# First units of a fused attention and FFN kernel: k copied in two parts, idle matmuls after k removed, intra products ahead of inter products, one natural-k group made last

## The chip, the core and the metric

The kernel runs on one core of one Trainium2 chip. Times are device microseconds (us) of whole executions; a profiled execution has a span (first to last instruction) about 1.7 us shorter than its time. A comparison is given as a median of each kernel and as a ratio.

## The reference

```
# attention: batch 4, 8 heads, 768 positions, head size 64, blocks of 64
intra = (qb @ kb^T) * Dmask          # decay lam^(i-j) below the diagonal
out   = intra @ vb + (qb * lam_pow) @ kv_state
kv_state = lam_block * kv_state + (kb * rev_pow)^T @ vb
# bilinear FFN on the result, x = [3072, 512]
y = ((x @ w_a) * (x @ w_b)) @ w_out  # d_ff = 1536
```

The kernel works in blocks ("units") of 128 positions, 24 of them, and folds the decay into q and k. Groups of one to four units go through the FFN together. The first group has four units, and its attention has to be finished before the FFN can begin. That stretch, the first 20 us, is called the head here.

## The kernel before

In the head, q and k of four units arrive in two loads each. VectorE (DVE) multiplies a load by its decay table in two parts, TensorE (PE) transposes each part with four matmuls against an identity, and ScalarE (ACT) copies the result out of PSUM:

```python
    def load4(w, i):
        ...
        tps = ps_bank("t" + w, [128, 2, PACK, 128], BF16)     # one PSUM bank
        for j in range(2):
            ...                                               # DVE multiplies part j
            for r in range(PACK):
                nc.tensor.transpose(tps[:, j, r, :], ..., ident)
        nc.scalar.copy(xT4[w][:, 2 * i:2 * i + 2, :]..., tps[:]...)   # one copy, both parts
    ...
    for w in "qk":
        for i in range(2):
            load4(w, i)
            warm(4)                       # four idle matmuls
    ...
    scores4(0)                            # q k products; DVE masks follow
    natural_k(0, "act")                   # k transposed back, four units, heads 0-3
    natural_k(1, "act")                   # heads 4-7
    scores4(1)
    ...                                   # kv products of units 0-2, states copied out
    for u in range(n0):
        inter(u)                          # q times the state of the unit before
        intra(u)                          # masked scores times v
        evac_o(u, ...)                    # xT, which the FFN reads
```

`ps_bank` hands out seven PSUM banks in turn. The FFN's first matmuls, a_ps, read xT of all four units.

## Time and profile before

| | before |
|---|---|
| median of 3 runs | 238.19 us (237.91 to 238.54) |
| span of the profiled run | 236.1 us, mean granted clock 0.998 |
| first a_ps matmul | 20.06 us |
| PE busy from 20 to 40 us | 19.94 of 20 us |

The page's row of granted clock, in tenths over 40 slices of the span, is shown here:

```profile
PEclk9999999999999999999999999999999999999999
```

Each digit stands for 5.9 us; 9 is 90% or more. By this row TensorE ran at full clock from beginning to end. It leaves out both ends: the clock record in the packed trace begins only at 6.71 us, and until then the first idle matmuls, 512 columns wide, start 0.43 us apart, where those at full clock in the changed kernel start 0.22 apart; and the last 0.73 us, in which TensorE has no work, are at half clock, which is what takes the mean to 0.998.

### The profile page before, as it was taken

To read this page: it belongs to the slowest core of one execution; us is meant where nothing else is said; L and a number is where in the kernel's file an instruction comes from. 1 tells how busy PE (TensorE), PEld (TensorE's weight loads), DVE (VectorE), ACT (ScalarE), POOL (GpSimd) and SP (SyncE) were. 2 spreads that over 40 slices of the span, in tenths; PEclk is the share of its full clock that TensorE was granted. 3 is DMA by queue.
4 is the path that set the end of the run, shared out by engine and by line. 5 is a ranking of instruction groups with operands and counts; after the bars stand their busy time and mean duration, and the time that the engine had idled before them with its cause. 6 is when DMAs were issued, how large, how long until landed. Compare 5 with 4: busy or idle time off the path is not lost.

```text
span 236.1 us, 4532 instructions
## 1 busy us (share of the span) xinstructions
PE 227.6 (96%) x1769; PEld 126.3 (53%) x1769; DVE 116.5 (49%) x205; ACT 92.4 (39%) x171; POOL 48.8 (21%) x63
## 2 busy tenths in 40 slices
PE   7788999999999999999999999999999999999993
PEld 2474444449698654454544454544455544444493
DVE  0885665646558637665235567135474314331050
ACT  3576555055564542241142341233332333431161
POOL 6050000145345354103306403003300000000000
PEclk9999999999999999999999999999999999999999
DMA  4999999999999999996919869423020220000211
GB/s 159 297 292 349 351 365 287 284 213 287 230 208 205 220 184 250 238 181 100 246 74 217 169 104 216 126 90 76 16 47 0 89 90 3 0 0 26 110 44 49
DMA packets 94278, 38.32 MB, mean 162 GB/s; under 512 B 81200, under 2 KB 89776, under 8 KB 94256
## 3 DMA queue, kind: packets, MB, share of 16 engines
q1 hardware_dynamic: 94112, 38.02, 70.6%
q8 instruction: 14, 0.23, 0.4%
q14 instruction: 8, 0.07, 0.1%
q10 hardware_dynamic: 144, 0.00, 0.0%
HBM read 28.32 MB, written 6.29 MB: 147 GB/s over the span
## 4 chain that ended last, share of the span: by engine, by line
PE 90%; DMA 3%; ACT 2%; DVE 2%; issue 1%; SPq 1%; DVEq 0%
PE a_ps L405 27%; PE b_ps L405 26%; PE op L426 26%; DMA k<-in_k_dram 3%; PE o_ps L337 3%; PE kq L308 2%; PE kvd L351 2%; PE o_ps L329 2%; PE tps L294 1%; ACT scratch L515 1%; ACT o_sb L421 1%; SPq L206 1%; DVE scratch L495 1%; PE kv L351 0%; DVE m L320 0%
## 5 line engine op out<-in xcount | busy, mean ns | idle before, releaser
L417 DVE TENSOR_TENSOR ab<-a_sb,b_ps 128x512 bf16<-128x512 bf16 (+2 forms) x96 | 52.6, 552 | 81.6 <-PE b_ps L405 61.4
L405 PE MATMUL a_ps<-xT,wa_sb 128*128 128x512 bf16 (+2 forms) x384 | 77.1, 326 | 1.2 <-DVE wb_sb L161 0.7
L405 PE MATMUL b_ps<-xT,wb_sb 128*128 128x512 bf16 (+2 forms) x384 | 77.2, 326 | 0.0
L412 ACT CAST a_sb<-a_ps 128x512 bf16<-128x512 f32 (+2 forms) x96 | 45.5, 480 | 66.5 <-PE a_ps L405 66.1
L426 PE MATMUL op<-wo_sb,ab 128*128 128x512 bf16 (+2 forms) x312 | 65.6, 363 | 0.0
L405 PEld LDWEIGHTS <-wb_sb 128*128 128x128 bf16 x384 | 34.5, 98 | 28.6
L405 PEld LDWEIGHTS <-wa_sb 128*128 128x128 bf16 x384 | 33.6, 98 | 28.1 <-issue 1.5
L426 PEld LDWEIGHTS <-ab 128*128 128x128 bf16 x312 | 28.7, 98 | 30.1
L320 DVE TENSOR_TENSOR m<-kq,lotri 128x512 bf16<-128x512 f32 x48 | 29.9, 682 | 21.0 <-PE kq L308 19.8
L256 POOL TENSOR_TENSOR qk<-kf,lp_k 128x512 bf16<-128x512 f32 x17 | 17.9, 1051 | 78.1 <-issue 31.7
L421 ACT COPY o_sb<-op 128x512 f32<-128x512 f32 (+2 forms) x26 | 14.2, 553 | 37.2 <-PE op L426 37.2
L261 POOL TENSOR_TENSOR qk<-qf,lp_q 128x512 bf16<-128x512 f32 x20 | 22.5, 1127 | 24.4 <-DMA qf<-in_q_dram 24.4
L344 ACT CAST xT<-o_ps 128x512 bf16<-128x512 f32 x23 | 12.5, 589 | 16.9 <-PE o_ps L337 16.8
L373 DVE TENSOR_TENSOR st<-kvd,bdiag 128x512 bf16<-128x512 f32 x18 | 12.3, 683 | 3.8 <-PE kvd L351 3.8
L296 ACT COPY qkT<-tps 128x1024 bf16<-128x1024 bf16 x7 | 7.1, 1012 | 11.1 <-PE tps L294 11.1
L270 DVE CAST vb<-vf 128x512 bf16<-128x512 f32 x17 | 9.5, 561 | 0.0
L194 PE MATMUL idle<-idle_sb 128*128 128x128 bf16 (+1 forms) x29 | 7.2, 402 | 1.3 <-DVE idle_sb L189 1.3
L337 PE MATMUL o_ps<-m,vb 128*64 128x128 bf16 x192 | 8.2, 223 | 0.0
L270 POOL CAST vb<-vf 128x512 bf16<-128x512 f32 x7 | 4.3, 611 | 15.1 <-DMA vf<-in_v_dram 13.8
L329 PEld LDWEIGHTS <-st 128*128 128x128 bf16 x80 | 5.4, 98 | 3.0 <-ACT st L371 0.3
L337 PEld LDWEIGHTS <-vb 128*64 128x64 bf16 x192 | 5.8, 109 | 1.6
L308 PE MATMUL kq<-qkT 64*128 64x128 bf16 x160 | 6.6, 218 | 0.0
(52 smaller groups left out, 84.0 us busy)
## 6 DMA issues: line engine op xcount, KB each, us to landing
vf<-in_v_dram SPq DMA_DIRECT2D x24, 256.0 KB, 4.9
out_dram<-o_sb SPq DMA_DIRECT2D x23, 256.0 KB, 2.3
qf<-in_q_dram SPq DMA_DIRECT2D x20, 256.0 KB, 4.4
kf<-in_k_dram SPq DMA_DIRECT2D x20, 256.0 KB, 4.8
wst<-in_moe_w_a_dram SPq DMA_DIRECT2D x6, 512.0 KB, 8.7
wst<-in_moe_w_b_dram SPq DMA_DIRECT2D x6, 512.0 KB, 8.8
wst<-in_moe_w_out_dram SPq DMA_DIRECT2D x6, 512.0 KB, 8.5
q<-in_q_dram SPq DMA_DIRECT2D x2, 512.0 KB, 5.4
```

Source lines behind the costliest of these rows:

```text
L256: eng_of(eng).tensor_mul(qk[:, 1], raw.pop((u, "k")), lp_k[:, u % NB].to_broadcast([128, H, D]))
L261: eng_of(eng).tensor_mul(U[u]["qk"][:, 0], raw.pop((u, "q")), lp_q[:, u % NB].to_broadcast([128, H, D]))
L270: eng_of(eng).tensor_copy(vb, vf)
L320: nc.vector.tensor_mul(m, kq[i], lotri_bc)
L337: nc.tensor.matmul(d["o"][p, hp, :], lhsT=d["vb"][:, 2 * hp + i, :], rhs=d["m"](i, hp), start=(u % NB == 0 and hp == 0), stop=True, skip_g ...
L344: nc.scalar.copy(xT[:, :, col:col + BLK], o_ps)
L373: nc.vector.tensor_mul(st[:].rearrange("p hp i d -> p hp (i d)"), ps[:].rearrange("p hp i d -> p hp (i d)"), bdiag_bc)
L405: nc.tensor.matmul(ps[:, :gt], lhsT=w_sb[:, s, f * 128:(f + 1) * 128], rhs=xT[:, s, :gt], start=(s == 0), stop=(s == KS - 1))
L412: nc.scalar.copy(a_sb[:, :gt], ps[:, :gt])
L417: nc.vector.tensor_mul(ab[:, f, :gt], a_sb[:, :gt], ps[:, :gt])
L421: nc.scalar.copy(o_sb[:, lo:hi], op[:, lo:hi])
L426: nc.tensor.matmul(op[:, lo:hi], lhsT=ab[:, f, t * 128:(t + 1) * 128], rhs=wo_sb[:, f, lo:hi], start=(f == 0), stop=(f == FC - 1))
```

## The change

The intent is a shorter head. A load of k is copied out in two parts, so that ScalarE can start after four transposes; the idle matmuls after the k loads go; intra products, which need no state, come ahead of the inter products that wait for one; and the natural k of unit 3, which is needed last, is made after all else.

```diff
-    def inter(u):
-        d["o"] = ps_bank("o_ps", ...)
+    # inter and intra take the bank when they come first for a unit
...
+            if parts == 2:
+                unpack(i, tps, slice(j, j + 1), w)      # after each part, for k
+        if parts == 1:
+            unpack(i, tps, slice(0, 2), w)              # after both, for q
...
-    for w in "qk":
+    for w, parts in (("q", 1), ("k", 2)):
         for i in range(2):
-            load4(w, i)
-            warm(4)
+            load4(w, i, parts)
+            if w == "q":
+                warm(4)
...
-    natural_k(0, "act")
-    natural_k(1, "act")
+    natural_k((0, 1, 2), (0, 1))
+    natural_k((0, 1, 2), (2, 3))
...
-    for u in range(n0):
-        inter(u)
-        intra(u)
-        evac_o(u, *xTs[u], eng="dve" if u == 2 else "act")
+    intra(0)
+    evac_o(0, *xTs[0])
+    intra(1)
+    inter(1)
+    evac_o(1, *xTs[1])
+    intra(2)
+    intra(3)
+    inter(2)
+    evac_o(2, *xTs[2], eng="dve")
+    inter(3)
+    evac_o(3, *xTs[3])
+    natural_k((3,), (0, 1, 2, 3))
```

More of the change, by code (lines that the diff above doesn't have):

```diff
@@ L322, in mask, with o_bank @@
         return ms
+    def o_bank(u):
+        first = "o" not in U[u]
+        if first:
+            U[u]["o"] = ps_bank("o_ps", [128, HP, 128], F32)
+        return first
     def inter(u):
         d = U[u]
-        d["o"] = ps_bank("o_ps", [128, HP, 128], F32)
         if u % NB > 0:
+            first = o_bank(u)
             for hp in range(HP):
-                nc.tensor.matmul(d["o"][:, hp, :], lhsT=st_bufs[(u - 1) % 4][:, hp, :, :], rhs=d["qT"][:, hp, :],
-                                 start=(hp == 0), stop=False, skip_group_check=True)
+                nc.tensor.matmul(d["o"][:, hp, :], lhsT=st_bufs[(u - 1) % 4][:, hp, :, :],
+                                 rhs=d["qT"][:, hp, :], start=(first and hp == 0), stop=True,
+                                 skip_group_check=True)
     def intra(u):
         d = U[u]
+        first = o_bank(u)
         for hp in range(HP):
@@ L337, in intra @@
                 nc.tensor.matmul(d["o"][p, hp, :], lhsT=d["vb"][:, 2 * hp + i, :],
-                                 rhs=d["m"](i, hp), start=(u % NB == 0 and hp == 0),
+                                 rhs=d["m"](i, hp), start=(first and hp == 0),
                                  stop=True, skip_group_check=True)
@@ L487, with load4 @@
     kn4 = scr[1][:, 8:12, :].rearrange("p u (h d) -> p u h d", d=D)
-    def load4(w, i):
+    def load4(w, i, parts):
         dst = xs4[w].rearrange("p r (h d) -> p r h d", d=D)
@@ L501, in load4, with unpack, natural_k @@
                                     xs4[w][:, r, hs.start * D:hs.stop * D], ident)
+            if parts == 2:
+                unpack(i, tps, slice(j, j + 1), w)
         staged.pop((w + "4", i))
-        nc.scalar.copy(xT4[w][:, 2 * i:2 * i + 2, :].rearrange("c hp (p r) -> c hp p r", r=PACK),
-                       tps[:].rearrange("c j r p -> c j p r"))
-    def natural_k(i, eng):
-        tps = ps_bank("tn", [128, PACK, 2, 128], BF16)
-        for u in range(PACK):
-            for j in range(2):
-                nc.tensor.transpose(tps[:, u, j, :],
-                                    xT4["k"][:, 2 * i + j, u * BLK:(u + 1) * BLK], ident)
-        dst = kn4[:, :, 4 * i:4 * i + 4, :].rearrange("p u h d -> p u (h d)")
-        src = tps[:].rearrange("p u j x -> p u (j x)")
-        if eng == "act":
-            nc.scalar.copy(dst, src)
-        else:
-            nc.vector.tensor_copy(dst, src)
+        if parts == 1:
+            unpack(i, tps, slice(0, 2), w)
+    def unpack(i, tps, js, w):
+        nc.scalar.copy(xT4[w][:, 2 * i + js.start:2 * i + js.stop, :]
+                       .rearrange("c hp (p r) -> c hp p r", r=PACK),
+                       tps[:, js].rearrange("c j r p -> c j p r"))
+    def natural_k(us, hps):
+        nu, nh = len(us), len(hps)
+        tps = ps_bank("tn", [128, nu, nh, 128], BF16)
+        for a, u in enumerate(us):
+            for b, hp in enumerate(hps):
+                nc.tensor.transpose(tps[:, a, b, :], xT4["k"][:, hp, u * BLK:(u + 1) * BLK], ident)
+        nc.scalar.copy(kn4[:, us[0]:us[0] + nu, 2 * hps[0]:2 * (hps[0] + nh), :]
+                       .rearrange("p u h d -> p u (h d)"),
+                       tps[:].rearrange("p u j x -> p u (j x)"))
     ms4 = {}
```

## The prediction

> **What bounds the kernel now.** I read the page first. The chain that ended last is 90% TensorE and only 2% ScalarE, 2% VectorE and 3% DMA:
>
> ```profile
> PE 90%; DMA 3%; ACT 2%; DVE 2%; issue 1%; SPq 1%; DVEq 0%
> ```
>
> Next I asked for the busy time of each engine by stage, to see where TensorE (PE) has slack. This row has the stretch in us, its length, then busy time and instruction count of PE, PEld, DVE, ACT and POOL, the granted clock, DMA share and GB/s:
>
> ```profile
> 20.00:40.00 20.00, 19.94 (x96) 9.18 (x96) 11.64 (x19) 11.69 (x18) 0.00 (x0) 1.00 1.09 342
> ```
>
> PE is busy 19.94 of 20 us right after the head, and the waits of PE after 20 us add up to 1.2 us, of which 0.7 is the first one at 20 us itself. So from the first a_ps matmul on, PE is the bound, and the change touches nothing there. What it can do is move the start of that matmul, now at 20.06 us, and the end moves with it, one for one. Everything is decided between 8 and 20 us. There I read the chain of waits in order of time (start, length, what):
>
> ```profile
> 10.32 1.31 DVE scratch L495 x2
> ...
> 11.67 0.40 PE tk L500 x4
> 12.07 0.22 PE idle L194 x4
> 12.29 0.55 PE kq L530 x16
> 12.84 0.57 PE tn L510 x8
> ...
> 13.43 1.94 ACT scratch L515 x2
> 15.37 0.48 PE kv L351 x6
> ```
>
> and, because that chain puts a wait for several semaphores on the one that came last, the timeline beside it:
>
> ```profile
> 9.02 1.01 ACT L503 COPY scratch<-tq 128x1024 bf16<-128x1024 bf16 x1 [0.36 <-PE tq L500]
> 9.56 0.40 PE L500 MATMUL tk<-ident,scratch 128*128 128x128 bf16 x4 [0.35 <-DVE scratch L495]
> 10.60 1.01 ACT L503 COPY scratch<-tk 128x1024 bf16<-128x1024 bf16 x1 [0.56 <-PE tk L500]
> 12.72 4.87 DVE L320 TENSOR_TENSOR m<-kq,lotri 128x512 bf16<-128x512 f32 x8 [1.11 <-PE kq L530]
> 15.36 0.49 PE L351 MATMUL kv<-vb,scratch 128*128 128x128 bf16 x6 [0.31 <-ACT scratch L515]
> 17.19 0.23 PEld L329 LDWEIGHTS <-st 128*128 128x128 bf16 x4 [0.15 <-ACT st L371]
> 17.96 0.40 PE L329 MATMUL o_ps<-scratch,st 128*128 128x128 bf16 x4
> 18.96 0.41 PE L337 MATMUL o_ps<-m,vb 128*64 128x128 bf16 x8
> 19.42 0.59 ACT L344 CAST xT<-o_ps 128x512 bf16<-128x512 f32 x1 [0.41 <-PE o_ps L337]
> 20.06 1.89 PE L405 MATMUL a_ps<-xT,wa_sb 128*128 128x512 bf16 x8 [0.68 <-DVE wb_sb L161]
> ```
>
> The reader is to see four things. First, the eight masks run back to back on DVE: starts 0.60 us apart (4.87 less one of 0.68, by 7), each with a duration of 0.68 us. Second, the kv matmuls are credited to ACT's natural-k copies, but the built program lets the first of them wait for the fourth mask too (its bank) and only for the first natural-k copy. That copy ended near 14.4; the fourth mask at 12.72 + 3 x 0.60 + 0.68 = 15.2. So kv starts because of mask four, 2.64 us after mask one, not because of ACT. Third, from 15.36 to 19.37 PE works almost without gaps: 24 kv matmuls, then intra and inter. Fourth, a_ps is credited to the cast of wb_sb, which it does not read; what it needs is the last xT copy, 19.42 + 0.59 = 20.01. The true chain is: k multiplied, transposed, scores, masks one to four, kv, intra/inter, xT of unit 3.
>
> [...]
>
> **The change part by part.**
>
> *k unpacked in two parts.* Two copies of 1024 columns become four of 512, about 0.59 us each by the xT casts. The intent is that copying starts after four transposes, not eight. But in the program as built the first transpose of a load's second part waits for ACT's copy of its first part, as they share a bank. So transposes and copies of one load alternate. By the trace, ACT starts 0.44 us after the first of four transposes (10.16 to 10.60), and PE starts about 0.05 after an ACT end (20.01 to 20.06). Step by step, with DVE unchanged:
> - load 0, part 0: transposes 9.56; copy 10.00 to 10.59 (ACT's q copy ends at 10.03, overlap allowed).
> - part 1: transposes at 10.64 in place of 10.16; copy 11.08 to 11.67. Before, the whole copy ended at 11.61: nothing won.
> - load 1, part 0: transposes 11.07; ACT is taken until 11.67[...]; copy 11.58 to 12.17.
> - part 1: transposes at 12.21 in place of 11.67, 0.54 later.
>
> *Idle matmuls after k removed.* Four stood between the last transposes and the scores: from 11.67 the scores started 0.55 later (12.22). Without them only four transposes at 56 ns stand before, 0.23. The scores start at 12.21 + 0.23 = 12.44, so +0.22 us against 12.22. Mask one moves from 12.72 to 12.94, and kv from 15.36 to 15.58.
>
> *Natural k of three units.* Eight transposes and 1024 columns become six and 768, twice: 0.80 us a copy[...]. The second ends at about 15.05, before 15.36. That frees ACT by 0.3 us, but kv waits for mask four. Worth nothing now. The third group (four transposes, one copy of 0.59) comes after unit 3's inter products, beside the 0.64 us of the last xT copy, and its own copy runs from 20.1 to 20.7 where ACT was idle until 21.12. Its reader comes at 22.6. No cost.
>
> *Intra before inter.* Before, PE went intra 0 (16.78), inter 1 (17.19), intra 1 (17.52), inter 2 (17.96). Eight intra matmuls take 0.34 where nothing waits (18.29 to 18.63), so inter 1 waited 17.19 - 17.12 = 0.07 for its state, inter 2 17.96 - 17.86 = 0.10. The new order puts other intra products before both: -0.17 us. Checked with everything shifted by 0.22: intra 0 at 17.00, intra 1 17.34, inter 1 17.68 (state 0 at 17.38), intra 2 18.01 (mask eight ends at 17.82), intra 3 18.35, inter 2 18.69, inter 3 19.02 (state 2 at 18.42). No new wait. Last copy at 19.02 + 0.45 = 19.47, a_ps at 20.11.
>
> Sum: +0.54 - 0.32 - 0.17 = +0.05 us on 238.19, so 238.2.
>
> **The rivals.** (a) The bank wait costs less than I think, and mask one starts 0.3 us earlier than reckoned, since without the serial wait the removed idle matmuls would give 0.32: then about 237.7. For it: that is the intent. Against it: the wait stands in the program. (b) The alternation costs more: without overlap on ACT and with longer latencies each hand-over grows by 0.1, three hand-overs lie on the path, and mask eight then holds up intra 2: about +0.4, 238.6. (c) The clock falls since eight idle matmuls are gone. Gaps would stay under 0.8 us (11.47 to 12.21)[...], so it is unlikely; half speed over the 4 us of kv and intra/inter would add at most 4 us: 242. (d) The rotation of banks moves by one, as there is one more natural-k bank. The first a_ps then takes a bank that ACT's state copies released at about 18.1; no wait, no change.
>
> **Range and chances.** The three runs before spread over 0.63 us, more than the effect. From -0.5 by (a) to +0.4 by (b), with 0.2 of noise on either side: 237.5 to 238.9. Two per cent is 4.8 us; the window from the first k product to a_ps is 11 us, and no path in it shrinks or grows by half. Faster 0.005, same 0.985, slower 0.01.
>
> **What would show it.** In the profile after: second-part transposes of k starting just behind an ACT end (10.6 and 12.2); mask one at 12.9; kv 2.64 us behind it; no wait of the inter loads for ACT; a_ps at 20.1; the stretch after it as long as before. I am wrong if second-part transposes start at 10.2 and 11.7, if the matmuls of the head show a clock under 1, or if a_ps comes before 19.7 or after 20.6.

Figures of the trace before that bear on these steps: a copy takes 1.01 us at 1024 columns and 0.59 at 512; the two natural-k copies of 1.01 to 1.02 us take 1.93 together, so neighbours overlap by about 0.10; six kv matmuls of 128 columns take 0.33 us to the start of the next block (15.36 to 15.69), 55 ns each. The 0.80 us for 768 columns and the copy from 11.58, while ACT is taken until 11.67, are estimates. In the profile of f_natural_only two copies of 768 columns take 1.50 us together, 0.80 each with that overlap. That a low clock is unlikely with gaps under 0.8 us was the author's estimate too; no trace had shown it. In the clock record of that trace, which begins at 6.71 us, a half clock stands only in the last 0.73 us.

## The result

The changed kernel took 238.65 us (238.46 to 239.18, 4 runs) against 238.05 (237.83 to 238.54, 4 runs) for the one before; the ratio is 1.0026, 95% interval 1.0002 to 1.0049. That is 0.6 us longer, which counts as the same by the 2% rule and is within the range on record, but not for the reasons on record. The profiled run was 239.18 us, span 237.5, mean clock 0.983. Its page has these two rows, the granted clock and the chain that ended last by engine:

```profile
PEclk9959999999999999999999999999999999999998
...
PE 89%; ACT 3%; DMA 3%; issue 1%; DVE 1%; SPq 0%; DVEq 0%; ACTq 0%
```

One slice of the clock row reads 5 where all read 9 before. In the stretches (columns as in the prediction; the clock is the third number from the end) its edges are sharp:

```profile
10.60:10.80 0.20, 0.10 (x2) 0.10 (x2) 0.20 (x1) 0.05 (x1) 0.00 (x0) 1.00 1.39 221
10.80:11.00 0.20, 0.20 (x4) 0.11 (x2) 0.20 (x2) 0.00 (x0) 0.00 (x0) 0.60 1.29 209
11.00:11.20 0.20, 0.20 (x3) 0.07 (x2) 0.20 (x2) 0.00 (x0) 0.00 (x0) 0.50 1.17 192
...
17.40:17.60 0.20, 0.20 (x4) 0.20 (x3) 0.20 (x1) 0.00 (x0) 0.20 (x1) 0.50 1.09 353
17.60:17.80 0.20, 0.20 (x6) 0.20 (x4) 0.20 (x1) 0.00 (x0) 0.18 (x1) 0.83 1.09 353
```

0.60 in the second row means that the halving came 0.04 us into it, at 10.84; 0.83 in the last puts the return at 17.67. For 6.83 us, right through the head, TensorE had half its clock. The timeline of the head shows what that did:

```profile
10.06 0.58 ACT L517 COPY scratch<-tk 128x512 bf16<-128x512 bf16 x1
10.70 1.04 PE L508 MATMUL tk<-ident,scratch 128*128 128x128 bf16 x8 [0.67 <-ACT scratch L517]
11.22 1.14 ACT L517 COPY scratch<-tk 128x512 bf16<-128x512 bf16 x2 [0.57 <-PE tk L508]
12.41 0.59 PE L508 MATMUL tk<-ident,scratch 128*128 128x128 bf16 x4 [0.67 <-ACT scratch L517]
12.93 1.04 PE L542 MATMUL kq<-scratch 64*128 64x128 bf16 x16
13.64 4.88 DVE L320 TENSOR_TENSOR m<-kq,lotri 128x512 bf16<-128x512 f32 x8 [1.96 <-PE kq L542]
16.27 0.80 PE L359 MATMUL kv<-vb,scratch 128*128 128x128 bf16 x6
...
19.50 1.56 ACT L352 CAST xT<-o_ps 128x512 bf16<-128x512 f32 x3
...
21.12 1.89 PE L413 MATMUL a_ps<-xT,wa_sb 128*128 128x512 bf16 x7 [0.45 <-ACT xT L352]
```

Second-part transposes wait for ScalarE, as reckoned: the profile names it as the releaser at 10.70 and 12.41. But sixteen score matmuls now have a busy time of 1.04 us where they had 0.62, mask one is at 13.64 in place of the 12.94 reckoned (12.72 before), and the first a_ps at 21.12, 1.06 behind the kernel before. From there the two traces keep that distance to 72 us; another 0.2 us is lost at 75, and the last 0.1 at the end.

### The profile page after: what moved, and what is told of

It is laid out like the page before. It is cut to its first block, busy times and chain, and to the rows that moved or that the text cites. A ratio compares the mean times of both kernels' runs of the same rounds, so it can differ in the third digit from the quotient of the medians.

```text
span 237.5 us, 4496 instructions
## 1 busy us (share of the span) xinstructions
PE 226.4 (95%) x1738; PEld 127.5 (54%) x1761; DVE 115.4 (49%) x205; ACT 92.6 (39%) x174; POOL 48.4 (20%) x63
## 4 chain that ended last, share of the span: by engine, by line
PE 89%; ACT 3%; DMA 3%; issue 1%; DVE 1%; SPq 0%; DVEq 0%; ACTq 0%
PE a_ps L413 27%; PE b_ps L413 26%; PE op L434 26%; DMA q<-in_q_dram 3%; PE o_ps L345 2%; PE kq L308 2%; PE kvd L359 2%; PE o_ps L335 1%; PE tps L294 1%; ACT scratch L517 1%; ACT xT L352 1%; PE kq L542 1%; ACT o_sb L429 1%; PE tn L526 1%; DVE scratch L503 1%
## 5 line engine op out<-in xcount | busy, mean ns | idle before, releaser
L434 PE MATMUL op<-wo_sb,ab 128*128 128x512 bf16 (+2 forms) x300 | 64.3, 362 | 0.9 <-issue 0.5
L261 POOL TENSOR_TENSOR qk<-qf,lp_q 128x512 bf16<-128x512 f32 x20 | 22.0, 1099 | 23.9 <-DMA qf<-in_q_dram 23.9
L359 PEld LDWEIGHTS <-qk 128*128 128x128 bf16 x64 | 4.9, 98 | 2.9
```

Source lines behind the costliest of these rows:

```text
L261: eng_of(eng).tensor_mul(U[u]["qk"][:, 0], raw.pop((u, "q")), lp_q[:, u % NB].to_broadcast([128, H, D]))
L434: nc.tensor.matmul(op[:, lo:hi], lhsT=ab[:, f, t * 128:(t + 1) * 128], rhs=wo_sb[:, f, lo:hi], start=(f == 0), stop=(f == FC - 1))
```

## The experiments

**Two theories to begin with.** Clock theory: the idle matmuls had kept the clock up; without them, and with TensorE waiting for ScalarE between the parts, the clock falls to half (0.50 in the profile above; three of four executions had a mean under 0.996), and that is the loss. Hand-over theory: the wait on the shared bank is all of the loss, and the clock a detail of one run.

To compare heads between runs in which the k load landed at slightly different times, I take the time from the start of DVE's product of the second k load (10.32 us in the profile before) to the first a_ps matmul. The table gives this for every profile, with TensorE's wait for DVE near 58 us (its use comes later), the times, and how many executions of those timed had a mean clock below 0.996.

| kernel | product to a_ps | wait near 58 | median us (before) | ratio, 95% interval | clock under 0.996 |
|---|---|---|---|---|---|
| before | 9.74 | 0.3 | | | 3 of 33 |
| changed, profile at 0.983 | 10.74 | 0.3 | 238.65 (238.05) | 1.0026, 1.0002 to 1.0049 | 3 of 4 |
| after_again, profile at 0.997 | 9.51 | 1.1 | 238.49 (238.29) | 1.0019, 0.9996 to 1.0043 | 4 of 6 |
| a_idle_back | 9.73 | 0.6 | 238.12 (238.10) | 0.9986, 0.9952 to 1.0020 | 0 of 6 |
| b_no_idle | 9.52 | 0.9 | 238.79 (238.10) | 1.0007, 0.9972 to 1.0043 | 3 of 6 |
| g_split_only, profile at 0.993 | 10.71 | 0.7 | 238.84 (238.10) | 1.0020, 0.9984 to 1.0056 | 1 of 6 |
| e_order_only | 9.23 | 1.0 | 237.61 (238.10) | 0.9957, 0.9918 to 0.9997 | 0 of 6 |
| d_fill | 9.50 | 0.6 | 238.11 (238.29) | 0.9992, 0.9973 to 1.0010 | 0 of 6 |
| c2_two_banks | 9.00 | 0.3 | 237.13 (238.29) | 0.9957, 0.9937 to 0.9976 | 0 of 6 |
| i_order_idle0 | 9.00 | 0.3 | 237.78 (238.29) | 0.9975, 0.9953 to 0.9998 | 0 of 6 |
| f_natural_only | 9.74 | 0.7 | 238.30 (238.08) | 0.9986, 0.9948 to 1.0024 | 0 of 6 |
| j_early_product | 9.74 | none | 237.51 (238.08) | 0.9961, 0.9923 to 0.9998 | 0 of 6 |
| k_banks_early | 9.00 | none | 236.84 (238.08) | 0.9941, 0.9897 to 0.9985 | 1 of 6 |
| l_banks_early_idle | 9.00 | none | 236.44 (238.20) | 0.9938, 0.9888 to 0.9988 | 1 of 6 |

The 33 executions of the kernel before are those whose clock is listed one by one. Three of them are outliers at 238.97, 240.54 and 240.84 us, with clocks of 0.992, 0.990 and 0.993. The last two are among the runs of the kernel before that some comparisons use, and widen their intervals: 240.84 in those of a, b, g, e, f, j and k, 240.54 in that of l.

### a_idle_back: the idle matmuls put back

```diff
-            if w == "q":
-                warm(4)
+            warm(4)
```

> The changed kernel with the four idle matmuls put back after each k load. Clock theory (the head of the changed kernel runs at half clock in some executions because the idle matmuls are gone): no execution with a mean clock below 0.996, scores about 0.55 us behind the start of the last k transposes (near 12.8 us), mask one near 13.3, first a_ps near 20.4, time 238.4, so a little faster than the changed kernel though it has more work on TensorE. Rival, hand-over theory (all of the loss is the wait for the shared bank, the clock is a detail of one run): the idle matmuls only add 0.3 us, so 238.9.

No execution of six was below 0.998 and the median was 238.12, better than the 238.4 expected and far from the 238.9 of the rival. Two lines of its timeline:

```profile
13.23 4.88 DVE L320 TENSOR_TENSOR m<-kq,lotri 128x512 bf16<-128x512 f32 x8 [1.61 <-PE kq L542]
...
20.05 1.46 PE L413 MATMUL a_ps<-xT,wa_sb 128*128 128x512 bf16 x5 [0.45 <-ACT xT L352]
```

Mask one is where I put it (13.3), half a microsecond behind the kernel before, yet a_ps comes at 20.05 and not at 20.4. So the stretch from mask to a_ps gains more than I had reckoned; e_order_only shows why. With more work on TensorE the kernel was faster than the changed one, which speaks for the clock, though the two were timed in different rounds and the intervals of their ratios overlap.

### b_no_idle: only the idle matmuls removed

```diff
             load4(w, i)
-            warm(4)
+            if w == "q":
+                warm(4)
```

> The kernel before without the four idle matmuls after each k load, nothing else changed. Clock theory: in a part of the executions the mean clock is below 0.996, and those are 0.3 to 1 us slower than the others; median between 237.8 and 238.6. Rival: the clock stays, the scores start at 11.9 in place of 12.2, mask one at 12.4, first a_ps near 19.75, time 237.75 in all executions.

Half the executions had a clock of 0.991 to 0.994. But the rest of the expectation missed. The median, 238.79, is above the 237.8 to 238.6 expected, and the low clock did not make an execution slower: these took 238.63 to 238.97, and the three at 1.0 took 237.87, 238.77 and 239.00. In the profiled one, at full clock, a_ps came 0.22 us earlier than before, and the run still ended late, since TensorE waited 0.9 us for DVE near 58 us. That is another loss, taken up below.

### g_split_only: only the copy in two parts

```diff
+            if w == "k":
+                unpack(i, tps, slice(j, j + 1), w)
...
-        nc.scalar.copy(xT4[w]..., tps[:]...)
+        if w == "q":
+            unpack(i, tps, slice(0, 2), w)
```

> The kernel before with only k's copy in two parts; idle matmuls, order and natural k as before. Hand-over theory: second-part transposes at 10.64 and 12.2, scores near 12.75, mask one near 13.25, first a_ps near 20.6, time +0.5 against before (238.6); clock unchanged as the idle matmuls stay. Rival (the wait on the bank is short or hidden): mask one at 12.7, time 238.05.

The transposes came at 10.66 and 12.21 and the scores at 12.74, as expected. The rest was not: this profile fell in an execution whose clock halved from 12.68 to 16.09, although the idle matmuls were there, and mask one came at 13.46 and a_ps at 21.05. Yet this execution, at 238.62, was the second fastest of the six; the five without a low mean clock took 238.61 to 239.64, and nothing says where they lost it. Why the clock fell in this execution and not in others is not shown. The two profiles with a halving in the head have one distance in common. The thirteen wide idle matmuls at the very start start 0.43 us apart until TensorE speeds up (0.22 in the changed kernel), which the clock row does not show. That moment is where the clock record of the trace begins, and it differs between executions: 6.71 us in the profile before, 4.01 in that of the changed kernel and 5.85 in this one. In the two with a halving in the head, the halving comes 6.83 us after it (10.84 and 12.68), and it lasts 6.83 us in the one and 3.41 in the other. Idle matmuls outside the waits make a halving rare, not impossible; a and g, which have the same k stage, show it in 1 of 12 executions. The price of the split at full clock comes from two other profiles: a_idle_back has all parts but the removal of the idle matmuls, and with natural k worth nothing (below) its 9.73 less the 9.23 of e_order_only gives 0.50 us.

### e_order_only: only the order of intra and inter

```diff
-    for u in range(n0):
-        inter(u); intra(u); evac_o(u, ...)
+    intra(0); evac_o(0); intra(1); inter(1); evac_o(1)
+    intra(2); intra(3); inter(2); evac_o(2); inter(3); evac_o(3)
```

> The kernel before with only the order of intra and inter changed. My reckoning: the two waits for state copies (0.07 and 0.10 us) go, mask one stays at 12.7, first a_ps near 19.9, time 237.9. Rival (ScalarE is the bound there: four state copies and three xT copies in a row): first a_ps stays at 20.06, time 238.05.

The gain is three times what I expected, 9.74 to 9.23, and the median is 237.61 (237.9 expected). TensorE's timeline in the kernel before:

```profile
16.78 0.41 PE L337 MATMUL o_ps<-m,vb 128*64 128x128 bf16 x8
17.19 0.40 PE L329 MATMUL o_ps<-scratch,st 128*128 128x128 bf16 x4
17.52 0.41 PE L337 MATMUL o_ps<-m,vb 128*64 128x128 bf16 x8
...
18.29 0.41 PE L337 MATMUL o_ps<-m,vb 128*64 128x128 bf16 x8
```

and with the new order:

```profile
16.90 0.64 PE L345 MATMUL o_ps<-m,vb 128*64 128x128 bf16 x16
17.47 0.40 PE L335 MATMUL o_ps<-scratch,st 128*128 128x128 bf16 x4
17.80 0.64 PE L345 MATMUL o_ps<-m,vb 128*64 128x128 bf16 x16
18.37 0.62 PE L335 MATMUL o_ps<-scratch,st 128*128 128x128 bf16 x8
```

Sixteen intra matmuls in a row take 0.57 us from start to the next block, not twice the 0.34 of eight. Eight more cost 0.23, so about 0.11 of the 0.34 belongs to the block and not to its matmuls. Four inter matmuls take 0.33, and at the 55 ns of a 128-column matmul (six kv matmuls in 0.33 us) 0.22 of it is work: 0.11 again. So each change between the two forms (64-column and 128-column weights) seems to cost about 0.11 us, an estimate from these block times. The old order has seven blocks, the new four: 3 x 0.11 = 0.33, and with the 0.17 us of waits that I had counted, 0.50. The measured gain is 0.51. The rival, ScalarE as the bound, is out: it expected the first a_ps to stay at 20.06, and it came at 19.66.

### after_again: the changed kernel once more

No edit; the same kernel in six more executions.

> The changed kernel itself once more, for its clock in more executions. Clock theory: most executions show a mean clock below 0.996 (one window of 3.4 us at half speed takes 0.007 off the mean, two take 0.014), none of the executions of the kernel before in these rounds does so as often; where the profile falls in an execution without the half clock, mask one is at 12.95 and the first a_ps at 19.75, and such executions take about 237.8. Rival: the time does not go with the clock, the head is as long with and without.

The 3.4 us are the length of the halving in the profile of g_split_only (3.41 us, mean clock 0.993; half of it, in a span of 237 us, is the 0.007); two such stretches are the 6.83 us of the first profile of the changed kernel (0.983). For executions without a trace, one or two halved stretches are read off the mean clock alone.

Four of six were below 0.996 (0.984, 0.993, 0.982, 0.993); with the first four executions that makes seven of ten, against three of 33 for the kernel before. This time the profile fell in an execution at full clock, and the head is the one reckoned: mask one at 13.05, kv at 15.68, a_ps at 19.88. From product to a_ps it takes 9.51 us, 0.23 less than before. Against the first profile the half clock costs 10.74 - 9.51 = 1.23 us of head.

One part of the expectation missed. The two executions with two halved stretches took 238.95 and 239.85, but the ones at full clock took 238.59 and 238.39, no less than those with one (238.14, 238.37), and not 237.8. With the first four executions it is the same: by their mean clocks, the three of ten with two stretches took 238.95 to 239.85, the four with one 238.14 to 238.74, the three at full clock 238.39 to 238.59. So one halved stretch cannot be seen in the time, and the changed kernel is not faster than the one before even where the clock holds. Where the profiled one lost its lead shows in DVE's and GpSimd's (POOL) timeline:

```profile
56.69 1.47 DVE L256 TENSOR_TENSOR qk<-kf,lp_k 128x512 bf16<-128x512 f32 x1
...
56.58 1.04 POOL L256 TENSOR_TENSOR qk<-kf,lp_k 128x512 bf16<-128x512 f32 x1 [2.54 <-ACT a_sb L420]
```

and in the list of TensorE's waits from 55 to 60 us (total, times, longest):

```profile
PE a_ps L413 <- DVE ab L425: 1.1, 1, 1.1
```

The same two engines at this place in the kernel before:

```profile
56.87 0.68 DVE L256 TENSOR_TENSOR qk<-kf,lp_k 128x512 bf16<-128x512 f32 x1
...
55.94 1.04 POOL L256 TENSOR_TENSOR qk<-kf,lp_k 128x512 bf16<-128x512 f32 x1 [2.16 <-DMA kf<-in_k_dram]
56.94 1.52 POOL L261 TENSOR_TENSOR qk<-qf,lp_q 128x512 bf16<-128x512 f32 x1
```

The DVE product of 128x512 takes 0.68 us alone. Here, where a POOL product was under way, it is stretched to 1.47: it ends at 58.16, about 0.5 us behind the end of POOL's at 57.62. In a_idle_back and b_no_idle, where POOL's had begun 0.58 and 0.24 us before, it takes 1.01 and 1.36. In the kernel before it was POOL's second product that was stretched, 1.52 for 1.04, since DVE came first. In both cases the time is close to that of one product after the other: a second product that waited for all of the first would end at 58.30 and 58.59, and they end at 58.16 and 58.46. What makes them hinder each other, the traces do not show. POOL's product starts when its k load lands or when ScalarE releases it, DVE's when TensorE gets there: the first does not move with the head as the second does (POOL's at 55.50 and 56.58, DVE's at 57.94 and 56.69 in the first and second profile of the changed kernel), so who comes first changes from run to run and with every shift of the head. In the profiles of the kernel before and of after_again the wait near 58 us is 0.3 and 1.1 us. In the first profile of the changed kernel, with the half clock, DVE came late enough to find POOL done (0.69 us from 57.94), so that the two profiles of this kernel, 1.23 us apart at the head, end only 0.6 us apart.

### d_fill: idle matmuls inside the wait

```diff
                 unpack(i, tps, slice(j, j + 1), w)
+                if j == 0:
+                    warm(6)
```

> The changed kernel with six idle matmuls between the two parts of each k load, in the time in which TensorE waits for ScalarE to free the bank anyway. Clock theory: no execution below 0.996, scores at 12.45, mask one at 12.95, kv at 15.6, first a_ps at 19.75, time 237.8, faster than the changed kernel by 0.8. Rival (the bank wait alone is the loss): as slow as the changed kernel, 238.6, or slower.

The sharpest test: the changed kernel with its waits filled. Nothing that matters moved, as its timeline shows:

```profile
12.22 0.38 PE L508 MATMUL tk<-ident,scratch 128*128 128x128 bf16 x4 [0.38 <-ACT scratch L519]
...
13.04 4.88 DVE L320 TENSOR_TENSOR m<-kq,lotri 128x512 bf16<-128x512 f32 x8 [1.39 <-PE kq L544]
...
19.86 1.67 PE L413 MATMUL a_ps<-xT,wa_sb 128*128 128x512 bf16 x6 [0.45 <-ACT xT L352]
```

The head (9.50) is that of the changed kernel at full clock, and in six executions the clock was never below 0.999. The mean of these six is 238.05 us, that of after_again in the same rounds 238.72. The fill is therefore worth about 0.66 us here, with a standard error of 0.3 from the scatter of the two sixes. Not all of it need be the clock: the executions of after_again at full clock took 238.59 and 238.39, and the wait near 58 us was 0.6 in this profile and 1.1 in that one. Against the kernel before the filled one is 0.2 faster (ratio 0.9992), but the interval holds 1. The 237.8 expected was missed by 0.3; the wait near 58 us (0.6 in its profile) is a likely reason. The rival, which expected 238.6 or more, is out.

### f_natural_only: only the natural k of unit 3 made last

```diff
-    natural_k(0, "act")
-    natural_k(1, "act")
+    natural_k((0, 1, 2), (0, 1))
+    natural_k((0, 1, 2), (2, 3))
...
+    natural_k((3,), (0, 1, 2, 3))
```

> The kernel before with only the natural k of unit 3 made last. My reckoning: mask one stays at 12.7, kv at 15.35, since kv waits for mask four and not for the natural-k copies; first a_ps at 20.05; time as before. Rival (the profile's own reading, that ScalarE's natural-k copies release kv): kv starts up to 0.4 us earlier, at 15.0, and a_ps at 19.7.

The head is 9.74, to the hundredth that of the kernel before. The timeline settles who releases kv:

```profile
13.25 1.50 ACT L512 COPY scratch<-tn 128x768 bf16<-128x768 bf16 x2 [0.21 <-PE tn L511]
...
15.29 0.49 PE L351 MATMUL kv<-vb,scratch 128*128 128x128 bf16 x6 [0.31 <-DVE m L320]
```

ScalarE is now done at 14.75, and kv starts at 15.29 all the same, 2.64 us behind mask one (12.65). The profile, which credited ScalarE before, now names the mask.

### c2_two_banks: a bank for each part

```diff
-        tps = ps_bank("t" + w, [128, 2, PACK, 128], BF16)
+        if parts == 1:
+            tps = ps_bank("t" + w, [128, 2, PACK, 128], BF16)
         for j in range(2):
+            if parts == 2:
+                tps = ps_bank("t" + w, [128, 2, PACK, 128], BF16)
...
-            if w == "q":
+            if w == "q" or i == 0:
                 warm(4)
```

> The changed kernel with a PSUM bank for each part of a k load, and the four idle matmuls kept after the first k load. Hand-over theory: second-part transposes at 10.2 and 11.7 as before the change, scores at 11.9, mask one at 12.4, kv at 15.05, first a_ps at 19.25 (-0.8), time 237.3. Rival: mask one is no earlier than 12.7 because the copies of the first load end no earlier.

With a bank of its own the second part does not wait for the copy of the first:

```profile
10.02 1.19 ACT L520 COPY scratch<-tk 128x512 bf16<-128x512 bf16 x2
10.19 0.40 PE L511 MATMUL tk<-ident,scratch 128*128 128x128 bf16 x4 [0.21 <-DVE scratch L506]
...
19.34 1.89 PE L413 MATMUL a_ps<-xT,wa_sb 128*128 128x512 bf16 x7 [0.45 <-ACT xT L352]
```

The transposes follow DVE, as in the kernel before the change, while ScalarE is copying (10.02 to 11.21). The head is 9.00, 0.51 better than that of the changed kernel at full clock, which is the price of the shared bank once more. The median is 237.13, ratio 0.9957: better than both kernels. The first load's copies do not hold up mask one (12.52), so the rival is out.

### i_order_idle0: new order, k in one part

```diff
-            warm(4)
+            if w == "q" or i == 0:
+                warm(4)
 # and the new order of intra and inter, as in e_order_only
```

> The kernel before with the new order of intra and inter, without the idle matmuls after the second k load; k copied in one part, natural k as before. If the split and the third natural-k group are worth nothing, this equals the two-bank kernel: scores at 11.95, mask one at 12.45, first a_ps at 19.3, time 237.3. If the natural-k copies of four units hold kv up, kv starts at 15.1 or later and a_ps comes at 19.4 to 19.6.

The head is 9.00, the same as with two banks; a_ps at 19.47 is later only because the k load landed 0.13 us later. So in the head the split and the third natural-k group are worth nothing even where the split does no harm. The time, 237.78, is above the 237.3 expected, with executions from 236.88 to 238.26; the profiled one was the 236.88 and had no long wait near 58 us. What the others lost is not in a trace. This kernel, c2 and k (below) keep idle matmuls after the first k load alone, and 1 of their 18 executions had a low clock; of b and the changed kernel, which keep none, 10 of 16. This suggests that the four after the first load are the ones that matter for the clock, though these kernels differ in more than that.

### j_early_product: one DVE instruction moved ahead

```diff
-    1: [..., (2, "T", 5), (3, "PK", 6), ...]
+    1: [..., (2, "T", 5), (2, "PK", 6), ...]
```

In the built program the order changes on no engine but DVE, where the k product of unit 6 moves ahead of one FFN product.

> The kernel before with one VectorE instruction moved ahead by one place: the k product of unit 6 (near 57 us) comes before the third product of the FFN's second group, so that it starts near 55.4 us, while GpSimd is idle. [...] theory (in many executions that product waits for a GpSimd product under way, up to 0.8 us, and TensorE with it): its duration is 0.68 us, TensorE's wait for VectorE near 58 us goes, median 0.2 to 0.5 us below before, and less spread. Rival (the waits near 57 us are noise of the trace): time as before.

```profile
55.42 0.68 DVE L256 TENSOR_TENSOR qk<-kf,lp_k 128x512 bf16<-128x512 f32 x1
```

It runs in 0.68 us, POOL's product starts at 56.38, and TensorE's wait for DVE is gone from the list. The median is 237.51 against 238.08, a little more than the 0.2 to 0.5 expected, with six executions within 0.65 us of each other. What was expected of the early product holds.

### k_banks_early and l_banks_early_idle: both together

k is c2 with j's edit. l is k with `warm(4)` after the first part of each k load, where TensorE waits for DVE.

> The two-bank kernel (a bank for each part of a k load, idle matmuls kept after the first k load) with the same VectorE instruction moved ahead. If the two gains add: first a_ps at 19.3, no wait near 58 us, time 236.8 to 237.0, against 237.13 for the two-bank kernel alone. Rival: equal to the two-bank kernel, as its profile showed no wait near 57 us.

> The two-bank kernel with the early VectorE product, and four more idle matmuls between the two parts of each k load, where TensorE waits 0.3 us for VectorE anyway. Clock theory: they cost nothing (mask one at 12.5, first a_ps at 19.3) and no execution shows a mean clock below 0.996, where one of six of the kernel without them did (0.985, 239.04 us); median 236.8. Rival: a halved clock is as frequent with them, or they push the second-part transposes back and a_ps comes 0.1 us or more later.

The gains add: 236.84 for k, 236.44 for l, ratios 0.9941 and 0.9938, the fastest kernels here. The idle matmuls cost nothing in l (a_ps 19.33). But the claim that they rule out a low clock missed: one of its six executions had 0.993 and took 238.91, as one of k had 0.985 and took 239.04. Since only means are known for executions without a trace, where in them the clock fell stays open, and so it does for the three of the kernel before.

## Why the prediction was right, and where it was wrong

The time held, 238.2 with a range of 237.5 to 238.9 for a measured 238.65. It held partly by luck: the head came out shorter than reckoned, and two losses that the sum did not have, the half clock and the wait near 58 us, made up for it. By its own steps:

- **What bounds the kernel.** Right: kv follows mask one by 2.63 or 2.64 us in every head at full clock, f_natural_only showed that ScalarE does not release it, and a shift of a_ps passes through undiminished to 48 us in every profile. But "the end moves with it, one for one" is wrong: near 58 us, and a little near 75, the shift meets other waits, near 58 the one for POOL's product. The 0.18 us that the head of after_again was ahead became 0.61 behind there.
- **k in two parts, +0.54.** Right in mechanism and size: 0.50 from a_idle_back less e_order_only, and 0.51 from c2_two_banks.
- **Idle matmuls removed, -0.32.** The sign was right, the size was not: 9.74 to 9.52 in b_no_idle, -0.22. The scores do not follow the last transposes after 0.23 us but after 0.33 (11.68 to 12.01). What the step left out is that these matmuls were doing something, which is the next to last point.
- **Natural k of three units, 0.** Right: 9.74 in both.
- **Intra before inter, -0.17.** Mechanism incomplete, size wrong: -0.51. I took the time of a block as that of its matmuls and counted waits only; by the estimate above the change of form costs 0.11 us each, and three changes went. The numbers to see it were in the kernel before, whose chain has sixteen intra matmuls of a later group in 0.57 us beside eight in 0.34.
- **The sum, +0.05.** With the measured terms it is 0.50 - 0.22 - 0.51 + 0 = -0.23, what after_again's profile shows at full clock (9.51 against 9.74). The 0.50 comes from a kernel that has the new order too, so this checks only that the idle matmuls add; the 0.51 from c2_two_banks is a second measure of it.
- **Rival (c), the clock.** This is the step that failed: "it is unlikely", because gaps stay under 0.8 us, was an estimate. The gap behind each hand-over was as I said (0.67 us), but seven of ten executions had a clock below 0.996. In the 3.41 us ahead of the halving the longest gap was 0.67 us in the changed kernel and 0.71 in g_split_only. In the first profile of the changed kernel TensorE was busy for 2.02 us of that stretch (7.43 to 10.84); in that of after_again, which kept its clock, for 2.04 of the same one. The gap of 0.67 us is in both. So neither the gaps nor the busy time of these profiles tell when the clock falls. The half clock cost 1.23 us of head in the profiled one. What it costs on average is not settled: filling the waits won 0.66 with a standard error of 0.3, yet within the ten executions of the changed kernel only the three with two halved stretches are slower. The rest of the way from -0.2 to +0.6 is likely the wait near 58 us, as in the traced execution at full clock, but executions without a trace cannot show its share.
- **What would show it wrong.** Two of the marks that I had set came up in the first profile: a clock under 1 in the head, and a_ps after 20.6.

Shown by runs are the four terms, the cost of the half clock in the head, its absence in six executions with filled waits, and the wait near 58 us with its cure. Argued only: that a block's 0.11 us comes from the change of weight form as such, and how the measured 0.6 us divides between the half clock and the wait near 58 us.

## What to carry to other kernels

An "idle" instruction may be there for what it does to the clock (here under 0.996 in 3 of 33 executions of the kernel before and in 7 of 10 of the changed one): before removing one, look whether a wait opens there, and if so try to fill it: here that cost nothing (9.50 us of head against 9.51), and the clock held in all six executions of d_fill, if only in five of six of l. TensorE writing a PSUM bank and ScalarE reading it take turns here even when they touch different halves (in the changed kernel TensorE is idle for 0.67 us until ScalarE releases the second part at 10.70; with two banks it transposes from 10.19, while ScalarE copies from 10.02 to 11.21; 0.51 us of head), so a copy split in two wants two banks. It can pay to keep matmuls of one form together (0.51 us for the new order here), and a gain at the front of a kernel can be lost to a wait behind it (in after_again 0.18 us ahead at a_ps, 0.61 behind near 58 us).
